# Attention and SoLU layer on one core: the output product with 16-bit words in place of 32-bit ones

## The chip, the cores and the metric

The kernel runs on one core of one Trainium2 chip. The metric is device microseconds of one execution, from the first to the last instruction and what lies around them. A run gives one time; the median of three runs stands for the kernel.

## The reference, cut to what matters

Eight batches of eight heads of causal attention with a decay (576 positions, head size 64) give `x`, 4608 tokens by 512. A layer follows, token by token:

```python
h = x @ w_in                      # 512 -> 1024
e = exp(h - max(h)); sm = e / (sum(e) + 1e-9)
solu = h * sm
ln = (solu - mean(solu)) / sqrt(var(solu) + 1e-6) * g_ln
out = ln @ w_out                  # 1024 -> 512
```

Inputs and output are 32-bit floats. `q` and `k` are scaled so that the scores spread widely, and the result must be near that of 32-bit arithmetic.

## The kernel before, in words

The 4608 tokens are 36 tiles of 128, called layers 0 to 35 here. The attention of eight batches, four pairs of heads each, feeds them through `xt`, a buffer of two batches. A layer (`layer`, L663) does this in order: TensorE multiplies `xh`, `xl` with `wi_h`, `wi_l` (L676 to L678, 24 matmuls of 512 columns into `hps`); VectorE takes the row's maximum (L687), ScalarE the exponential (L688), VectorE weighs and sums (L692 to L695), ScalarE squares for the variance (L700), GpSimd makes the inverse deviation in two small instructions (L704, L705), and the row is centred. The normalised row `z` must be transposed before the second product. Layers 5 to 29 (`turned`) have it as two 16-bit words, written by L318 and L714, transposed by DMA into `zz16` and then converted to two 32-bit words `zh` and `zl` by a ScalarE copy (L316, through `copied`) and a VectorE copy (L318), two halves each. Layers 0 to 4 and 30 to 35 transpose the 32-bit row on TensorE (L726) and split it on the way out of PSUM: `zh` by ScalarE (L734), `zl` by VectorE (L735). In these the row is only centred (L718); the inverse deviation is applied to the output (L776, L767), so that L718 does not wait for L705.

The second product (`product_out`, L743 to L745) takes three matmuls for each of eight blocks of 128 hidden units: `zh` with the high word of W_out, `zh` with its low word, `zl` with the high word; all operands are `float32r`, 128 by 128 stationary and 512 columns moving. That is 24 matmuls a layer. The last layer does it in two halves of 256 columns (L756, L757, L759).

W_out comes in as four tiles of 64-bit floats (`prepare_w_out`, L428; `weights`, L387): each is loaded, made into 32-bit floats by L409, L411 and a copy, and then every block of 128 rows is multiplied by its `g_ln` and split into `wo(0, k)` (through `copied`) and `wo(1, k)` (L439), block by block, as soon as its own tile is there. The 32-bit tile lies in `zt` or in a buffer of the attention (`w_buffer`). W_in goes through the same helper earlier.

The order on every engine is set once, when the program is built, by `Plan.schedule`: each operation has an engine, a cost in ns, a due time and keys that it reads and writes; of what is ready on an engine the one with the least due time goes first, within a short window (`WAIT`). Due times are a priority, not a clock. A matmul group needs a slot of PSUM: two each of `s` (scores), `t` (transposes), `o` (outputs). Engines run their order strictly; on the chip an instruction that waits holds back all behind it. All DMAs are issued by SyncE's queue (L322, L325). Where the plan leaves TensorE idle in its first 140 us and after 690 us, short 16-bit matmuls of a constant (L832, 256 columns) fill the time.

Of the kernel before, what the change touches and what calls it, by code (L numbers as in the profile page):

```python
# [18 lines left out]
P = 128  # L19
# [19 lines left out]
COLUMN, TRANSPOSE = 0.4525, 109.0  # L39
# [143 lines left out]
DUE = dict(load=-29.542, split=-28.082, upper=-25.473, v=-9.217, S=((-17.447, -8.873), (-8.986, -3.876), (-5.065, -1.009), (-2.23, 0.228), (-0.2, 2.951)), T=((-3.123,), (-2.859,), (2.11, 1.41), (11.821, 15.242), (13.671, -6.196, 17.385)), V=((15.498, 10.925), (22.811, 25.245)))  # L183
EARLY = dict(load=-47.636, split=-34.061, upper=-50.243, v=-30.564, S=((17.018, -28.783), (6.139, -25.484), (-23.782, -37.469), (19.88, -8.857), (6.983, 36.241)), T=((16.416,), (-36.513,), (8.628, 2.588), (20.731, -15.249), (-3.969, 15.962, 16.559)), V=((-14.112, -16.964), (35.156, 1.04)))
PAIR = 23.13
C_OUT = 56.244
START = 86.713
HALF = ((28.5, 0.126), (52.37, -6.098))
# [3 lines left out]
AT_P, AT_L = (-12.344, -0.643, -5.355, 1.678, 0.284, 4.447, 0.791, -2.369, 8.072, 3.467, 4.155, -6.961, 0.853, 3.12, 2.845, 2.503, -2.212, -3.177, 1.73, -1.504, 6.409, 1.012, 0.682, -2.76, -5.909, 3.11, -3.789, -9.069, -2.092, 8.061, -5.047, -4.728), (1.766, 17.998, -5.159, 17.233, 0.49, -2.325, -5.371, -4.319, -2.569, 0.3, 6.438, 6.85, -0.263, 5.808, -0.074, -4.855, -0.333, 0.475, 6.874, 4.872, 7.281, 9.093, -1.339, -8.226, -2.067, -5.356, -6.63, -2.031, -3.859, 16.597, -2.614, -2.295, 1.064, 4.109, 7.541, 10.907)  # L192
FIRST = 96.18

STAGES = (-7.935, 1.059, 6.086, 23.041, 12.213)
# [3 lines left out]
def tile_kernel(ctx: ExitStack, tc: tile.TileContext, qk, v, f, w_in, w_out, g_ln, out):  # L199
# [99 lines left out]
    st = [sb(f"st_{n}", 8) for n in range(2)]  # L299

# [86 lines left out]
    def weights(src, n, due, t, tk, w, wk, first=()):  # L387

        def words(x):
            return now(t).rearrange("p c (n t) -> p c n t", t=2)[:, :, :, x]  # L390
        dma(due + W_DMA[n // NCC] if n else -98, t, src.bitcast(I32).rearrange("p (c n) -> p c n", n=512), 712 if tk[0][0] != "xt" else 940, reads=first, writes=tk)
        w = w.rearrange("p (c n) -> p c n", c=4)
        wi = w.bitcast(I32)


        copied(W_UP[n], {ACT: 1140, POOL: 1150}, due, w, lambda: words(1).bitcast(F32), tk, [wk], scale=2.0 ** -112)
        for a in range(2):
# [8 lines left out]
            else:  # L406
# [10 lines left out]
    def prepare_w_in(c, due):  # L417
        w, wk = w_buffer(c % 3)
        weights(w_in[c], c, due, lambda: buf(f"wo_{c}", "raw", 4, DM, dtype=I32), [(("wo", "wol")[c // 2], 4 * (c % 2) + j) for j in range(4)],
                w, wk, summed if c else ())  # L420
        copied(WI_H[c], {ACT: 1050, DVE: 690, POOL: 1130}, due, wi_h[:, c, :], w, [wk], [("wi", c)])
        op(WI_L[c], 2360 if WI_L[c] == POOL else 1170, due, lambda: (nc.gpsimd if WI_L[c] == POOL else nc.vector).tensor_tensor(
            wi_l[:, c, :], w, wi_h[:, c, :].bitcast(F32), ALU.subtract), reads=[wk, ("wi", c)], writes=[("wil", c)], port=True)

    def wo(x, k):
        return buf(f"wo_{2 * x + k // 4}", "f32r", 4, DM, dtype=F32R)[:, k % 4, :]

    def prepare_w_out(c, due):  # L428
# [4 lines left out]
        w, wk = w_buffer(1 + c % 2)  # L433
        weights(w_out[c], NCC + c, due, t, tk, w, wk, summed)
        w = w.rearrange("p (r n) -> p r n", r=2)
        for r in range(2):
            k = 2 * c + r
            copied(WO_H[k], {ACT: 600, DVE: 400, POOL: 620}, due, lambda k=k: wo(0, k), w[:, r], [("g",), wk], [("wo", k)], scale=g_sb[:, k:k + 1])
            op(DVE, 650, due, lambda r=r, k=k: nc.vector.scalar_tensor_tensor(  # L439
                wo(1, k), w[:, r], g_sb[:, k:k + 1], wo(0, k).bitcast(F32), ALU.mult, ALU.subtract),  # L440
               reads=[("g",), wk, ("wo", k)], writes=[("wol", k)], port=True)


# [219 lines left out]
    def layer(n, at):  # L663
# [6 lines left out]
        s = st[n % 2]  # L670
# [32 lines left out]
        def deviation(by=2.0 ** -20 if turned else 1.0):  # L703
            nc.gpsimd.tensor_scalar(s[:, 6:7], s[:, 5:6], by / DFF, 1.0e-6 * by, ALU.mult, ALU.add)  # L704
            nc.gpsimd.tensor_tensor(s[:, 7:8], s[:, 6:7], mhalf, ALU.pow)  # L705
        op(POOL, 805, at if turned else at + 1.0, deviation, [("st5", n % 2)], [("st7", n % 2)])
# [8 lines left out]
        else:  # L715
            for a in range(2 if last else 1):
                sl, zk = (slice(512 * a, 512 * a + 512), ("z", a)) if last else (slice(0, DFF), ("z",))
                op(c_eng, {DVE: 360 if last else 690, POOL: 1200}[c_eng], at, lambda sl=sl: engine(c_eng).tensor_scalar(  # L718
                    zt[:, sl], et[:, sl], s[:, 4:5], 1.0, ALU.add, ALU.mult), [("e",), ("st", n % 2)], [zk], clear=[("z",)], port=c_eng == DVE)
        at += tz - tmid  # L720
        for a in range(2):
            key = ("t", "z", n, a)

            def turn(a=a, key=key):
                for k in range(4):
                    nc.tensor.transpose(ps_t[plan.place[key]][:, k, :], zt[:, (4 * a + k) * P:(4 * a + k + 1) * P], ident)  # L726
# [6 lines left out]
            op(PE, 4 * TRANSPOSE, at + 0.3 * a, turn, [("z", a) if last else ("z",)], [key], take=key, clear=[("zh", a), ("zl", a)])  # L733
            op(ACT, 470, at + 0.5, lambda a=a, key=key: nc.scalar.copy(zh[a], ps_t[plan.place[key]]), [key], [("zh", a)])  # L734
            op(DVE, 603, at + 1.0, lambda a=a, key=key: nc.vector.tensor_tensor(  # L735
                zl[a], ps_t[plan.place[key]], zh[a].bitcast(F32), ALU.subtract), [key, ("zh", a)], [("zl", a)])
# [3 lines left out]
        def product_out(k):  # L740
            o = ps_o[plan.place[key]]
            a, j = divmod(k, 4)
            nc.tensor.matmul(o, zh[a][:, j], wo(0, k), start=(k == 0), stop=False)  # L743
            nc.tensor.matmul(o, zh[a][:, j], wo(1, k), start=False, stop=False)  # L744
            nc.tensor.matmul(o, zl[a][:, j], wo(0, k), start=False, stop=(k == NFC - 1))  # L745

        if last:

            for b in range(2):
                ok, cols = ("o", "y", n, b), slice(256 * b, 256 * b + 256)  # L750

# [124 lines left out]
```

## Time and profile before

| | us |
|---|---|
| three runs, median | 795.7 |
| three runs, lowest and highest | 792.31, 798.37 |
| profiled execution, span from first to last instruction | 795.1 |
| TensorE busy | 780.0 |
| VectorE busy | 621.7 |
| ScalarE busy | 541.1 |
| GpSimd busy | 508.6 |

The profiled execution is one more execution with the profiler on; its span lies 0.6 us under the median of the runs. In the rows, PE is TensorE's matmuls, PEld its loads of the stationary operand, DVE VectorE, ACT ScalarE, POOL GpSimd, SP SyncE. A matmul's duration is its latency: matmuls overlap, so the time that one costs is the step from its start to the next one's start.

### The profile page before, as it was taken

The numbers are of one execution on the slowest core, as the hardware profiler recorded it, in microseconds if no ns is written. First come the engines' busy times: TensorE is split into PE (matmuls) and PEld (weight loads), VectorE is DVE, ScalarE is ACT, GpSimd is POOL, SyncE is SP. The second block draws the span as 40 slices with busy tenths as digits, with TensorE's granted clock in tenths as the row PEclk, the third lists the DMA queues.
The fourth block names the chain that finished last, engine by engine and source line by source line (L and its number), as shares of the span: only waits on it lengthen the run. The fifth ranks groups of instructions, "written<-read, shape, count | busy, mean of one in ns | idle before, by whom it ended". The sixth has DMA issues, their size and how long they took to land.

```text
span 795.1 us, 15849 instructions
## 1 busy us (share of the span) xinstructions
PE 780.0 (98%) x4763; PEld 660.6 (83%) x4763; DVE 621.7 (78%) x1902; ACT 541.1 (68%) x1367; POOL 508.6 (64%) x687
## 2 busy tenths in 40 slices
PE   8999999899999999999999999999999999999998
PEld 6667878788888888888888888888888888898887
DVE  6889878887878878988977878898879877885233
ACT  4565767876867777867766777776768776875343
POOL 4565667685668687758566787776767685752230
PEclk9899999999999999999999999999999999999999
DMA  8638577857476657766756666668476684520000
GB/s 269 202 115 233 156 195 201 217 163 192 120 184 152 159 147 188 181 148 164 181 148 165 148 168 152 159 159 205 122 194 137 153 181 123 118 49 14 27 27 27
DMA packets 117014, 120.08 MB, mean 151 GB/s; under 512 B 64000, under 2 KB 78592, under 8 KB 116160
## 3 DMA queue, kind: packets, MB, share of 16 engines
q1 hardware_dynamic: 116928, 119.06, 58.7%
q8 instruction: 38, 0.62, 0.4%
q14 instruction: 48, 0.39, 0.2%
HBM read 39.11 MB, written 10.03 MB: 62 GB/s over the span
## 4 chain that ended last, share of the span: by engine, by line
PE 85%; DVE 5%; DMA 3%; POOL 3%; issue 2%; ACT 1%; SPq 1%; POOLq 0%; DVEq 0%; ACTq 0%
PE ps_o L638 13%; PE ps_t L598 10%; PE hps L676 8%; PE ps_o L743 8%; PE hps L677 7%; PE hps L678 7%; PE ps_o L744 7%; PE ps_o L745 7%; PE ps L551 5%; PE ps L552 5%; PE hps L832 4%; DVE p L556 1%; POOL p L572 1%; PE ps_t L726 1%; PE ps L549 1%
## 5 line engine op out<-in xcount | busy, mean ns | idle before, releaser
L572 POOL TENSOR_SCALAR p<-p,ri 128x320 f32<-128x320 f32 (+4 forms) x320 | 191.1, 611 | 95.7 <-DVE ri L568 83.6
L559 ACT ACTIVATE p<-p,nm 128x320 f32<-128x320 f32 (+4 forms) x320 | 178.0, 557 | 68.2 <-DVE nm L556 60.7
L606 DVE TENSOR_TENSOR ptl_f32r<-ps_t,pth_f32r 128x384 fp32r<-128x384 f32 (+3 forms) x272 | 137.2, 519 | 23.5 <-ACT pth_f32r L316 20.9
L316 ACT ACTIVATE pth_f32r<-ps_t 128x384 fp32r<-128x384 f32 (+3 forms) x272 | 120.7, 461 | 51.2 <-PE ps_t L598 46.6
L556 DVE CUSTOM_DVE_ANT_0 p<-ps,mask 128x320 f32<-128x320 f32 (+4 forms) x320 | 130.6, 422 | 26.1 <-PE ps L552 11.7
L598 PE MATMUL ps_t<-ident,p 128*128 128x128 f32 x800 | 128.0, 275 | 3.6 <-DVE ptl_f32r L606 1.9
L598 PEld LDWEIGHTS ps_t<-ident,p 128*128 128x128 f32 x800 | 97.0, 141 | 28.0 <-POOL p L572 5.4
L676 PE MATMUL hps<-wi_h,xh 128*128 128x512 f32 x288 | 118.6, 412 | 0.0
L743 PE MATMUL ps_o<-wo_f32r,zh 128*128 128x512 f32 x280 | 117.3, 419 | 0.0
L677 PE MATMUL hps<-wi_l,xh 128*128 128x512 f32 x288 | 113.7, 395 | 0.0
L678 PE MATMUL hps<-wi_h,xl 128*128 128x512 f32 x288 | 113.6, 394 | 0.0
L551 PE MATMUL ps<-ks_f32r,qs_f32r 128*128 128x320 f32 (+3 forms) x360 | 110.5, 316 | 2.2 <-DVE nm L556 1.4
L744 PE MATMUL ps_o<-wo_f32r,zh 128*128 128x512 f32 x280 | 110.7, 396 | 0.0
L745 PE MATMUL ps_o<-wo_f32r,zl 128*128 128x512 f32 x280 | 110.5, 395 | 0.0
L552 PE MATMUL ps<-kz_f32r,qz 128*128 128x320 f32 (+3 forms) x360 | 102.9, 297 | 0.7 <-DMA kz_f32r<-raw 0.5
L638 PE MATMUL ps_o<-pth_f32r,vs_f32r 128*128 128x256 f32 (+1 forms) x368 | 94.4, 268 | 0.0
L672 POOL TENSOR_TENSOR xl<-xt,xh 128x512 fp32r<-128x512 f32 x36 | 46.5, 1293 | 57.5 <-ACT xh L671 56.7
L551 PEld LDWEIGHTS ps<-ks_f32r,qs_f32r 128*128 128x128 f32 (+1 forms) x360 | 65.0, 181 | 13.9 <-DVE nm L556 5.7
L638 PE MATMUL ps_o<-ptl_f32r,vs_f32r 128*64 128x256 f32 (+1 forms) x368 | 71.4, 264 | 0.0
L638 PEld LDWEIGHTS ps_o<-pth_f32r,vs_f32r 128*128 128x128 f32 x368 | 70.1, 191 | 1.6
L552 PEld LDWEIGHTS ps<-kz_f32r,qz 128*128 128x128 f32 (+1 forms) x360 | 65.3, 181 | 6.3 <-DMA kz_f32r<-raw 1.1
L678 PEld LDWEIGHTS hps<-wi_h,xl 128*128 128x128 f32 x288 | 54.1, 188 | 13.0
(137 smaller groups left out, 1611.6 us busy)
## 6 DMA issues: line engine op xcount, KB each, us to landing
raw<-in_qk_dram SPq DMA_DIRECT2D x64, 288.0 KB
ks_f32r<-hi SPq DMA_DIRECT2D x128, 144.0 KB
raw<-in_v_dram SPq DMA_DIRECT2D x32, 288.0 KB
kz_f32r<-raw SPq DMA_DIRECT2D x64, 144.0 KB
out_dram<-y SPq DMA_DIRECT2D x35, 256.0 KB
qs_f32r<-hi SPq DMA_DIRECT2D x56, 144.0 KB
qs_f32r<-raw SPq DMA_DIRECT2D x56, 144.0 KB
qz<-hi SPq DMA_DIRECT2D x56, 80.0 KB
```

The costliest lines, as they stand in the source:

```text
L551: nc.tensor.matmul(dst, qs(p)[:, h, q0:q0 + nq], ks(p)[:, h, cols], start=True, stop=False)
L552: nc.tensor.matmul(dst, z[:, h, z0:z0 + nq], kz(p)[:, h, cols], start=False, stop=True)
L559: op(ACT, E_NS[i], at + 1.3, lambda: nc.scalar.activation(pr, pr, AF.Exp, bias=x, scale=-1.0, accum_out=sm[m][i][:nq, h, 0:1]), [("nm", m, ...
L572: op(POOL, N_NS[i], at + 2.8, lambda g=g, pg=pg: nc.gpsimd.tensor_scalar(pg, pg, r_[:, g:g + 1], 1.0, ALU.mult, ALU.mult), [("ri", m, i)], ...
L598: nc.tensor.transpose(tp[:, s, :], pt[i][:, k * P:(k + 1) * P], ident)
L638: nc.tensor.matmul(o[:mm, a:w], vv, mv, start=(j == 0 and x == 0), stop=(j == order[-1] and x == 0))
L676: nc.tensor.matmul(hps[:, sl], xh[:, c, :], wi_h[:, c, sl], start=(c == 0), stop=False)
L677: nc.tensor.matmul(hps[:, sl], xh[:, c, :], wi_l[:, c, sl], start=False, stop=False)
L678: nc.tensor.matmul(hps[:, sl], xl[:, c, :], wi_h[:, c, sl], start=False, stop=(c == NCC - 1))
L743: nc.tensor.matmul(o, zh[a][:, j], wo(0, k), start=(k == 0), stop=False)
L744: nc.tensor.matmul(o, zh[a][:, j], wo(1, k), start=False, stop=False)
L745: nc.tensor.matmul(o, zl[a][:, j], wo(0, k), start=False, stop=(k == NFC - 1))
```

## The change

W_out's two words and z's two words become fp16. W_out times `g_ln` is scaled by a power of two that is found on the chip from its largest magnitude, the output copy divides by it (`scales`), and z is normalised in every layer before it is transposed, so L718 now reads the inverse deviation. The DMA-transposed words are used by the second product as they land: `zh`, `zl` and the two copies in layers 5 to 29 are gone, and `zz16` has two sets, of even and odd layers. W_out's four 32-bit tiles stay in memory until the scale is known: only then (`scale_w_out`, new) are the eight blocks scaled and split. Costs and due times of the planner are new throughout.

```diff
-COLUMN, TRANSPOSE = 0.4525, 109.0
+COLUMN, TRANSPOSE, SHORT = 0.4525, 109.0, 0.4215
...
-PAIR = 23.13
-START = 86.713
-W_IN, W_OUT, LOAD = (-14.581, 46.719), (174.062, 72.91), (87.19, -12.196)
-W_DMA = (-132.187, -51.852)
+PAIR = 23.152
+START = 86.674
+W_IN = (-31.427, 49.165)
+W_OUT = (167.026, 57.23)
+LOAD = (91.563, -22.285)
+W_SCALE = 216.178
+W_DMA = (-107.022, -70.722)
...
-    zh, zl = ([sb(f"z{x}_{a}", 4, P, dtype=F32R) for a in range(2)] for x in "hl")
-    zz16 = [sb(f"zz16_{a}", 2, 4, P, dtype=F16) for a in range(2)]
+    zz16 = [[sb(f"zz16_{m}_{a}", 2, 4, P, dtype=F16) for a in range(2)] for m in range(2)]
...
     def wo(x, k):
-        return buf(f"wo_{2 * x + k // 4}", "f32r", 4, DM, dtype=F32R)[:, k % 4, :]
+        return buf(f"wo_{2 + x}", "f16", NFC, DM, dtype=F16)[:, k, :]
...
-        w, wk = w_buffer(1 + c % 2)
-        weights(w_out[c], NCC + c, due, t, tk, w, wk, summed)
+        weights(w_out[c], NCC + c, due, t, tk, w, wk, summed, clear=[("raww", c // 2)])
+        op(DVE, 1200, due, lambda: nc.vector.tensor_reduce(
+            top[:, 2 * c:2 * c + 2], w().rearrange("p (r n) -> p r n", r=2), axis=AX.X, op=ALU.max, apply_absolute_value=True), [wk], [("top", c)])
+    def scale_w_out(due):
+        key = ("t", "scale")
+        def across():
+            nc.vector.tensor_tensor(top[:, :NFC], top[:, :NFC], g_sb, ALU.mult)
+            nc.vector.tensor_reduce(top[:, NFC:], top[:, :NFC], axis=AX.X, op=ALU.max, apply_absolute_value=True)
+        op(DVE, 320, due, across, [("g",), *(("top", c) for c in range(NFC // 2))], [("top",)])
+        op(PE, 150, due, lambda: nc.tensor.transpose(ps_t[plan.place[key]][:1, 0, :], top[:, NFC:], ident), [("top",), ("const",)], [key], take=key, dense=False)
...
+        op(DVE, 650, due, exponents, [key], [("scales",)])
+        op(PE, 150, due, lambda: nc.tensor.matmul(ps_t[plan.place[key]][:, 1, :2], ones, scales[:1, :], start=True, stop=True), [("scales",), ("ones",)], [key], dense=False)
...
+        op(DVE, 500, due, factors, [key, ("g",)], [("scales",), ("sg",)])
+        for k in range(NFC):
+            wk = ("w32", k // 2)
+            copied(WO_H[k], {ACT: 600, DVE: 400, POOL: 620}, due + k, lambda k=k: wo(0, k), lambda k=k: wo32(k), [("sg",), wk], [("wo", k)],
+                   scale=sg[:, k:k + 1], clear=[("raww", 2)])
+            op(DVE, 650, due + k, lambda k=k: nc.vector.scalar_tensor_tensor(
+                wo(1, k), wo32(k), sg[:, k:k + 1], wo(0, k), ALU.mult, ALU.subtract),
+               reads=[("sg",), wk, ("wo", k)], writes=[("wol", k)], clear=[("raww", 3)], port=True)
...
-        op(POOL, 805, at if turned else at + 1.0, deviation, [("st5", n % 2)], [("st7", n % 2)])
+        op(POOL, 805, at, deviation, [("st5", n % 2)], [("st7", n % 2)])
...
-                    zt[:, sl], et[:, sl], s[:, 4:5], 1.0, ALU.add, ALU.mult), [("e",), ("st", n % 2)], [zk], clear=[("z",)], port=c_eng == DVE)
+                    zt[:, sl], et[:, sl], s[:, 4:5], s[:, 7:8], ALU.add, ALU.mult), [("e",), ("st", n % 2), ("st7", n % 2)], [zk], clear=[("z",)], port=c_eng == DVE)
...
-                           [("z",), ("z", "l")], [("zz", a)])
-                copied(Z_ENG[2], {ACT: 560, DVE: 350, POOL: 600}, at + 0.5, zh[a], zz16[a][:, 0], [("zz", a)], [("zh", a)])
-                copied(Z_ENG[3], {ACT: 560, DVE: 350, POOL: 600}, at + 0.5, zl[a], zz16[a][:, 1], [("zz", a)], [("zl", a)])
+                           [("z",), ("z", "l")], zk)
...
-            nc.tensor.matmul(o, zh[a][:, j], wo(0, k), start=(k == 0), stop=False)
-            nc.tensor.matmul(o, zh[a][:, j], wo(1, k), start=False, stop=False)
-            nc.tensor.matmul(o, zl[a][:, j], wo(0, k), start=False, stop=(k == NFC - 1))
+            nc.tensor.matmul(o, zz[a][:, 0, j], wo(0, k), start=(k == 0), stop=False)
+            nc.tensor.matmul(o, zz[a][:, 0, j], wo(1, k), start=False, stop=False)
+            nc.tensor.matmul(o, zz[a][:, 1, j], wo(0, k), start=False, stop=(k == NFC - 1))
...
-            op(PE, 3 * 512 * COLUMN + 12, at + tout * k / 8, lambda k=k: product_out(k),
+            op(PE, 3 * 512 * SHORT, at + tout * k / 8, lambda k=k: product_out(k),
```

`exponents` is four VectorE instructions of one row, `factors` three small ones of 128 rows. The lists of due times (`DUE`, `EARLY`, `HALF`, `AT_P`, `AT_L`, `STAGES`) all have new values.

## Rows read from the trace of the kernel before

**Rows 1.** The page, part 1: busy time of each engine.

```profile
PE 780.0 (98%) x4763; PEld 660.6 (83%) x4763; DVE 621.7 (78%) x1902; ACT 541.1 (68%) x1367; POOL 508.6 (64%) x687
```

**Rows 2.** The page, part 4: the chain that ended last.

```profile
PE 85%; DVE 5%; DMA 3%; POOL 3%; issue 2%; ACT 1%; SPq 1%; POOLq 0%; DVEq 0%; ACTq 0%
```

**Rows 3.** Busy time by stretch: start:end length, PE, PEld, DVE, ACT, POOL, PEclk, DMA.

```profile
40.00:100.00 60.00, 59.14 (x378) 44.75 (x377) 51.72 (x144) 39.72 (x96) 37.26 (x52) 0.99 0.60 169
...
190.00:690.00 500.00, 497.18 (x3006) 427.18 (x3005) 413.68 (x1292) 361.45 (x933) 354.48 (x459) 1.00 0.65 159
742.00:786.00 44.00, 43.81 (x207) 35.51 (x206) 16.99 (x33) 18.21 (x31) 10.18 (x14) 1.00 0.05 19
```

**Rows 4.** Timeline of PE: from layer 32's output product to layer 34's input product.

```profile
755.24 0.40 PE L743 MATMUL ps_o<-wo_f32r,zh 128*128 128x512 f32 x1
...
760.14 0.40 PE L676 MATMUL hps<-wi_h,xh 128*128 128x512 f32 x1
```

**Rows 5.** Waits of PEld, 190 to 700 us: total, times, longest.

```profile
PEld ps_t L598 <- DVE ptl_f32r L606: 3.4, 8, 1.3
PEld ps L551 <- DVE nm L556: 3.4, 13, 0.8
```

**Rows 6.** Timeline of PE: 256 columns in 16-bit words, then in 32-bit ones.

```profile
66.57 2.68 PE L832 MATMUL hps<-ident 128*128 128x256 bf16 x23
...
412.47 0.28 PE L638 MATMUL ps_o<-pth_f32r,vs_f32r 128*128 128x256 f32 x1
...
412.82 0.28 PE L638 MATMUL ps_o<-ptl_f32r,vs_f32r 128*64 128x256 f32 x1
```

**Rows 7.** Instructions of line 832: ns min/median/max, first and last start.

```profile
L832 PE MATMUL hps<-ident x290: 270/273/421, 3.4 to 69.9; 128*128 128x256 bf16 x145
```

**Rows 8.** Instructions of line 743: ns min/median/max, first and last start.

```profile
L743 PE MATMUL ps_o<-wo_f32r,zh x280: 388/397/500, 99.5 to 783.6; 128*128 128x512 f32 x140
```

**Rows 9.** Groups by line and form: count, busy us, mean ns, idle before.

```profile
L687 DVE TENSOR_REDUCE st<-hps 128x1 f32<-128x1024 f32 x36 | 43.9, 1220 | 24.6 <-PE hps L678 24.3
...
L318 DVE TENSOR_SCALAR zl<-zz 128x512 fp32r<-128x512 f16 x50 | 32.5, 664 | 2.3 <-DMA zz<-z 1.9 <-PE ps_o L745 0.2
...
L316 ACT ACTIVATE zh<-zz 128x512 fp32r<-128x512 f16 x50 | 30.5, 627 | 11.1 <-DMA zz<-z 9.2 <-ACT e L688 1.0 <-PE ps_o L744 0.9
...
L695 DVE TENSOR_SCALAR st<-st 128x1 f32<-128x1 f32 x36 | 5.5, 154 | 1.5
```

**Rows 10.** Instructions of line 439: ns min/median/max, first and last start.

```profile
L439 DVE SCALAR_TENSOR_TENSOR wo_f32r<-ptl_w,g_sb,wo_f32r x4: 723/742/752, 58.1 to 77.0; 128x512 fp32r<-128x512 f32 x4
```

**Rows 11.** Timeline of all engines: the end of layer 34 and layer 35's chain.

```profile
775.62 0.69 DVE L735 TENSOR_TENSOR zl<-ps_t,zh 128x512 fp32r<-128x512 f32 x1 [4.32 <-ACT zh L734]
...
778.67 0.40 PE L743 MATMUL ps_o<-wo_f32r,zh 128*128 128x512 f32 x1
...
783.41 1.16 ACT L700 ACTIVATE p<-e,st 128x1024 f32<-128x1024 f32 x1 [2.01 <-DVE st L695]
783.48 0.88 DVE L718 TENSOR_SCALAR z<-e,st 128x512 f32<-128x512 f32 x2
...
784.28 1.03 PE L726 MATMUL ps_t<-ident,z 128*128 128x128 f32 x8
784.47 0.18 ACT L700 ACTIVATION_READ_ACCUMULATOR p<-e,st 128x1 f32 x1
...
784.74 0.19 POOL L704 TENSOR_SCALAR st<-st 128x1 f32<-128x1 f32 x1 [10.04 <-ACT p L700]
785.02 0.55 POOL L705 TENSOR_TENSOR st<-st,mhalf 128x1 f32<-128x1 f32 x1
...
785.84 0.39 PE L756 MATMUL ps_o<-wo_f32r,zh 128*128 128x256 f32 x1 [0.19 <-ACT zh L734]
```

**Rows 12.** Timeline of PE: layer 2's last output triple, layer 3's first.

```profile
181.58 0.48 PE L743 MATMUL ps_o<-wo_f32r,zh 128*128 128x512 f32 x1
...
194.28 0.39 PE L743 MATMUL ps_o<-wo_f32r,zh 128*128 128x512 f32 x1
```

More of the change, by code (lines that the diff above doesn't have):

```diff
@@ L198, in tile_kernel @@
+FIRST = 96.162
+STAGES = (1.419, 1.059, 4.523, 23.041, 11.635)
 @with_exitstack
@@ L383, in tile_kernel, with weights, w4, wi @@
     dma(-90, g_sb, g_ln, 4, writes=[("g",)])
-    def weights(src, n, due, t, tk, w, wk, first=()):
+    def weights(src, n, due, t, tk, w, wk, first=(), clear=()):
         def words(x):
             return now(t).rearrange("p c (n t) -> p c n t", t=2)[:, :, :, x]
+        def w4():
+            return now(w).rearrange("p (c n) -> p c n", c=4)
+        def wi():
+            return w4().bitcast(I32)
         dma(due + W_DMA[n // NCC] if n else -98, t, src.bitcast(I32).rearrange("p (c n) -> p c n", n=512), 712 if tk[0][0] != "xt" else 940, reads=first, writes=tk)
-        w = w.rearrange("p (c n) -> p c n", c=4)
-        wi = w.bitcast(I32)
-        copied(W_UP[n], {ACT: 1140, POOL: 1150}, due, w, lambda: words(1).bitcast(F32), tk, [wk], scale=2.0 ** -112)
+        copied(W_UP[n], {ACT: 1140, POOL: 1150}, due, w4, lambda: words(1).bitcast(F32), tk, [wk], scale=2.0 ** -112, clear=clear)
         for a in range(2):
@@ L418, in prepare_w_in @@
         w, wk = w_buffer(c % 3)
-        weights(w_in[c], c, due, lambda: buf(f"wo_{c}", "raw", 4, DM, dtype=I32), [(("wo", "wol")[c // 2], 4 * (c % 2) + j) for j in range(4)],
+        weights(w_in[c], c, due, lambda: buf(f"wo_{c}", "raw", 4, DM, dtype=I32), [("raww", c)],
                 w, wk, summed if c else ())
@@ L432, in prepare_w_out @@
             t, tk = buf("ptl_1", "raw", 256 * 9, dtype=I32)[:, :2048].rearrange("p (c n) -> p c n", c=4), [("ptl", 3), ("ptl", 4)]
-        w, wk = w_buffer(1 + c % 2)
-        weights(w_out[c], NCC + c, due, t, tk, w, wk, summed)
[L435 to L441, printed above, removed]
+        wk = ("w32", c)
@@ L763, in layer @@
                         for k in range(4 * a, 4 * a + 4):
[L764 to L765 removed]
+                            op(PE, (2 - x) * (256 * SHORT + 4), at + 3.0 * b + 0.1 * k, lambda k=k, x=x, product=product: product(k, x),
+                               [(("zh", "zl")[x], n % 2, a), ("wo", k)] if x else [("zh", n % 2, a), ("wo", k), ("wol", k)], [ok],
                                take=ok if k == 0 and x == 0 else None)
                 op(ACT, 360, at + 3.0 * b, lambda ok=ok, cols=cols: nc.scalar.activation(
[L768 removed]
+                    yt[:, cols], ps_o[plan.place[ok]][:, :256], AF.Copy, scale=scales[:, 0:1]), [ok, ("scales",)], [("y", b)], clear=[("y",)])
                 dma(at + 3.0 * b, out[n * P:(n + 1) * P, cols], yt[:, cols], 128, reads=[("y", b)])
@@ L771, in layer @@
         for k in range(NFC):
-            op(PE, 3 * 512 * COLUMN + 12, at + tout * k / 8, lambda k=k: product_out(k),
-               [("zh", k // 4), ("zl", k // 4), ("wo", k), ("wol", k)], [key], take=None if k else key)
+            op(PE, 3 * 512 * SHORT, at + tout * k / 8, lambda k=k: product_out(k),
+               [("zh", n % 2, k // 4), ("zl", n % 2, k // 4), ("wo", k), ("wol", k)], [key], take=None if k else key)
         at += tout
-        y = yt
-        op(ACT, 590, at, lambda: nc.scalar.activation(y, ps_o[plan.place[key]], AF.Copy, scale=2.0 ** -10 if turned else s[:, 7:8]),
-           [key, ("st7", n % 2)], [("y",)])
-        dma(at, out[n * P:(n + 1) * P, :], y, 256, reads=[("y",)])
+        op(ACT, 590, at, lambda: nc.scalar.activation(yt, ps_o[plan.place[key]], AF.Copy, scale=scales[:, 0:1]),
+           [key, ("scales",)], [("y",)])
+        dma(at, out[n * P:(n + 1) * P, :], yt, 256, reads=[("y",)])
     def half_of(p, half, at, due):
```

58 lines of the change are left out of this document (36 added, 22 removed).

## The prediction

> **What bounds the kernel now.** I read the busy times first: TensorE has 780.0 us of the 795.1 us span, VectorE 78% and the others less [rows 1]. Busy alone does not prove a bound here, since matmuls overlap, so the second view is the chain that ended last: 85% of it is TensorE, VectorE and DMA together 8% [rows 2]. The third is the table by stretch. Between 190 and 690 us TensorE is busy 497.2 of 500 us at full granted clock, VectorE 413.7, ScalarE 361.5, GpSimd 354.5; in the last stretch, after the attention has ended, TensorE is full and the others are mostly idle; only between 40 and 100 us does another engine come near, VectorE with 51.7 of 60 us [rows 3]. The fourth is the timeline, to see whether TensorE really streams: from 755.24 to 760.14 us there are 21 matmuls of 512 columns one after the other, 4.90 us, 233.3 ns each [rows 4]. Their latency of about 395 ns is not what they cost; the step is. The waits say the rest: what the loads of the stationary operand wait for VectorE between 190 and 700 us is 3.4 + 3.4 = 6.8 us in all [rows 5]. So from about 190 us on, a nanosecond off TensorE's steps is a nanosecond off the span; before that it is a matter of what else arrives.
>
> **The change, part by part.**
>
> *Output product.* 35 layers of 8 blocks run each of three lines 280 times (line 743's row: x280) [rows 8], 840 matmuls of 512 columns; the last layer adds 48 of 256. All change from 32-bit to 16-bit words. The trace has 16-bit matmuls, the fillers: 23 of them of 256 columns take 2.68 us, of which the last one's own latency is 0.27 us [rows 7], so 2.41 us / 22 = 109.5 ns a step [rows 6]. The 32-bit ones of 256 columns step 0.35 us / 3 = 116.7 ns [rows 6], and half of 233.3 is the same 116.7: the 32-bit cost goes by the column. If the 16-bit one goes by the column too, 512 cost 219.0 ns and 14.3 ns are saved; if it is a column per cycle at the granted 2.4 GHz (106.7 ns for 256) and 2.8 ns fixed, 216.1 ns and 17.2 ns. The upper end is 213.3 ns, cycles alone, 20.0 ns saved. I take 217 ns, 16.3 ns saved: 840 x 16.3 = 13.7 us and 48 x 7.2 ns = 0.35 us, 14.05 us in all (12.0 to 16.8). Not all of it shortens the span. Layers 0 to 2 are multiplied between 99.5 [rows 8] and 181.6 us [rows 12], where TensorE still waits now and then; I count half of their 72 x 16.3 ns as hidden, 0.6 us. Layer 34's product lies beside the last layer's chain on VectorE and ScalarE, which does not get shorter: 0.4 us hidden. That leaves -13.0 us.
>
> The Trainium skill (TensorE: Matmul & The Clock Gate, Back-to-back issue gap) gives 512 / 2.4 + 2.5 ns, 215.7 ns, for a matmul at the higher clock; 840 times 17.6 ns would be an estimate of 14.8 us. The fillers' 109.5 ns at 256 columns lie near its 109.2 ns; it says nothing of why the 32-bit ones step 17 ns wider.
>
> *z's copies in layers 5 to 29.* 50 ScalarE copies of 627 ns and 50 VectorE ones of 664 ns go [rows 9]: 31 and 33 us of work, 9% and 8% of what these engines do between 190 and 690 us [rows 3]. They are off TensorE's path, so the 31 and 33 us are not a gain. What they can give is a part of the waits that end on VectorE, at most 6.8 us [rows 5] and at least nothing, since a wait can pass to GpSimd's normalisation, which keeps its work. I take -3.0 us, a little under half. Each half of z is also ready one copy earlier, which nothing waits for while TensorE has other work.
>
> *W_out's preparation.* What is loaded, rebuilt and split is the same; ahead of the split come four maxima over 1024 elements, for which L687's 1220 ns is the nearest row, and nine small VectorE instructions near L695's 154 ns [rows 9]: 4.9 + 1.4 = 6.3 us more VectorE work, in a stretch where it is idle for 8.3 us of 60 [rows 3]. Two tiny TensorE operations wait between them. Behind the first, the transpose of the maxima, stands everything on TensorE if VectorE's maximum is late; the plan puts it where its input should be ready, and its due time of 216 lets almost anything go ahead. Between the two a slot of `t` is held, of which there are two; the attention's transposes would have one for a few us. The split used to follow each tile; now its 16 instructions stand behind the last tile. Before, the last low word was started at 77.0 us [rows 10] and first used after 99.5 us [rows 8], 22 us later. The new chain after the last tile is 1.2 us (maximum), some 3 us (scale, two crossings to TensorE), and eight low words of 0.742 us [rows 10], 5.9 us: 10 us if dense, 20 us if VectorE gives it every other slot. It fits, barely. The bounds are 0 (all in idle VectorE time) and +6.3 us (all exposed); I take +2.5, nearer to the lower end, as the stretch also waits for DMAs. The four W_out loads keep their size and their place behind `xt` and `ptl_1`; the 32-bit tiles no longer take `zt`, which frees a little, counted as nothing.
>
> *z normalised before the transpose (layers 0 to 4, 30 to 35).* L718 now waits for two small GpSimd instructions, 0.19 + 0.55 us [rows 11]. In layer 34 the first half's low word is ready at 775.62 + 0.69 = 776.31 us and used at 778.67 us, 2.4 us later [rows 11]: the delay of under 1 us is covered by the next layer's input product. What loses that cover is the last layer, with nothing behind it. Today its z starts at 783.48 us, beside the square (783.41); now it must wait for the square, its sum (784.65), and GpSimd's two, which end at 785.57. z's first half takes about half of L718's 0.88 us, so the transposes start near 786.2 instead of 784.28, and everything after them moves by 1.9 us [rows 11]. Bounds: 1.0 us if the plan finds an overlap, 2.3 if the crossing to VectorE is slow. I take +1.9 us.
>
> *Due times.* The whole order is new. Nothing in the trace prices it; I count nothing and widen the range.
>
> **Sum.** -13.0 - 3.0 + 2.5 + 1.9 = -11.6 us. From the span of 795.1 us that is 783.5 us; the median of the runs lies 0.6 us above the span, so 784.1 us. Within the forecast's own bounds: most gain -15.8 - 6.8 + 0 + 1.0 = -21.6 (774.1), least -11.0 - 0 + 6.3 + 2.3 = -2.4 (793.3).
>
> **The rivals.** (A measurement of this kernel tells about 1% from no change: below 787.7 us is faster, above 803.7 slower.)
>
> *W_out's words come late, one layer's product is displaced.* If they are ready only after 105 us or so, layer 0's 24 matmuls (24 x 217 ns = 5.2 us) leave a stretch that has room and are paid in one that has none: 784.1 + 5.2 = 789.3 us, the same within 1%. For it: the low priority and VectorE's load [rows 3]. Against it: 22 us of slack [rows 8, 10].
>
> *The width does not matter.* The step is set by something that both formats share, and the 16.3 ns do not appear: 784.1 + 13.0 = 797.1 us, the same. For it speaks that the fillers are 256 columns of a constant, not 512 of data, and that they ran where little else used the memory; against it the 116.7 against 109.5 ns [rows 6]. The Trainium skill (TensorE: Matmul & The Clock Gate, Weight-path perf modes) states that the array processes one element per cell per cycle regardless of the element's width, which would give just this; the trace's two steps at 256 columns differ by 7 ns, so it does not agree for 32-bit against 16-bit words.
>
> *Slower: the scale becomes a gate.* The chain over VectorE and TensorE gets its slots so late that the words are not there when layer 3 wants to multiply (194.3 us [rows 12]). Then the products of layers 0 to 2 are all displaced (15.6 us), the extra VectorE work is exposed in full (+3.8 over my value) and the relief is lost (+3.0): 784.1 + 22.4 = 806.5 us. The mechanism decides for slower from about the third displaced layer; with two it ends at 801 us. Against it: W_out's steps had low priority before too and were done by 77.7 us [rows 10].
>
> *Better than forecast.* All of the 6.8 us of waits go and the preparation hides: 784.1 - 3.8 - 2.5 = 777.8 us.
>
> **How the numbers follow.** Forecast 0.60 (nearly all of it faster), better 0.12, one layer displaced 0.14 (a quarter of it still under 787.7), width does not matter 0.07, gate 0.07. Faster 0.59 + 0.12 + 0.03 = 0.74; slower is the gate's 0.07 less the part of it with only two layers displaced, 0.06; the rest, 0.20, the same. The range that leaves out two in ten reaches from the better case's lower side to the forecast's upper bound: 775.5 to 793.0 us.
>
> **What would show it.** Right: the step of L743 to L745's successors near 217 ns while L676 to L678 stay at 233; no ScalarE or VectorE copy between the DMA transpose and the product; VectorE with some 33 us less work in a stretch like that of 190 to 690 us, about 381 of 500; the last split of W_out before the first output product, and that product near 100 us; the last layer's transposes about 2 us behind the square's end. Wrong: steps of 230 ns; a first output product past 110 us with fillers in its place; waits of TensorE's scale transpose or of attention transposes for a `t` slot; a granted clock below 1.00 after 60 us, which would double the cost of every step there; or waits on GpSimd that take up what VectorE gives back.

## The result and the profile after

The changed kernel took 784.23 us (median of 4 runs, 783.74 to 786.25) against 795.73 us: a ratio of 0.9858, 95% interval 0.9826 to 0.9889. The profiled execution has a span of 782.0 us, 13.1 us under that of before. The forecast was 784.1 us, faster. A time lies some 1.8 us above the span of its own execution (783.74 and 782.0 us here), so the profiled execution of the kernel before stands for about 796.9 us, 1.2 us above its median.

The page of the changed kernel, parts 1 and 4, answers to [rows 1, 2]:

```profile
PE 768.1 (98%) x4817; PEld 589.8 (75%) x4817; DVE 595.1 (76%) x1865; ACT 515.0 (66%) x1317; POOL 499.2 (64%) x688
...
PE 78%; DMA 8%; DVE 5%; SPq 3%; POOL 3%; issue 2%; ACT 1%; POOLq 0%; DVEq 0%; ACTq 0%
```

TensorE is as full as before; VectorE lost 26.6 us and ScalarE 26.1 us, less than the copies' 33 and 31. By stretch, the same view as [rows 3]:

```profile
40.00:100.00 60.00, 58.17 (x360) 41.32 (x358) 54.77 (x148) 36.80 (x90) 36.77 (x51) 1.00 0.67 189
...
190.00:690.00 500.00, 496.77 (x3090) 385.98 (x3089) 395.01 (x1281) 348.23 (x913) 348.02 (x462) 1.00 0.66 159
```

Between 190 and 690 us VectorE is 18.7 us lighter, not 33. In part that is because 2.8% more matmuls, and the work that belongs to them, now fit into the same 500 us (3090 against 3006). TensorE's timeline over layer 34's output product answers to [rows 4]:

```profile
765.86 0.38 PE L781 MATMUL ps_o<-wo_f,zz 128*128 128x512 f16 x1
...
771.04 0.27 PE L870 MATMUL ps_o<-ident 128*128 128x256 bf16 x1
```

Between these two starts lie 24 matmuls: 5.18 us / 24 = 215.8 ns each, where it was 233.3. The loads of the stationary operand between 190 and 700 us, as in [rows 5]:

```profile
PEld L781 <- issue: 4.9, 22, 0.3
PEld ps L590 <- DVE nm L595: 4.2, 17, 0.4
PEld L781 <- DMA zz<-z: 2.9, 4, 1.0
PEld ps_t L637 <- DVE ptl_f32r L645: 2.5, 8, 0.5
PEld ps_o L677 <- DVE xt L699: 1.9, 5, 0.6
```

Waits that end on VectorE are 8.6 us here (4.2 + 2.5 + 1.9). Before, the same three kinds were 7.3 us, the two lines of [rows 5] and this one:

```profile
PEld ps_o L638 <- DVE xt L660: 0.5, 2, 0.4
```

The product now waits four times for the DMA transpose itself. The end of the kernel, as in [rows 11]:

```profile
764.32 1.22 DVE L726 TENSOR_REDUCE st<-hps 128x1 f32<-128x1024 f32 x1 [6.27 <-PE hps L717]
764.75 1.07 ACT L772 CAST zz<-ps_t 128x512 f16<-128x512 f32 x2 [4.85 <-PE ps_t L765]
764.99 1.04 PE L870 MATMUL ps_o<-ident 128*128 128x256 bf16 x8
...
770.00 0.18 ACT L739 ACTIVATION_READ_ACCUMULATOR p<-e,st 128x1 f32 x1
...
770.54 0.55 POOL L744 TENSOR_TENSOR st<-st,mhalf 128x1 f32<-128x1 f32 x1
...
771.13 1.00 DVE L757 TENSOR_SCALAR z<-e,st 128x512 f32<-128x512 f32 x2 [2.22 <-POOL st L744]
...
773.07 0.28 PE L794 MATMUL ps_o<-wo_f,zz 128*128 128x256 f16 x1
```

z now starts after GpSimd's second small instruction (its wait, 2.22 us, names it). From the start of VectorE's maximum to the first output matmul this chain takes 773.07 - 764.32 = 8.75 us. Before, it started here and ended at 785.84 us [rows 11], 6.96 us later:

```profile
778.88 1.23 DVE L687 TENSOR_REDUCE st<-hps 128x1 f32<-128x1024 f32 x1 [1.43 <-PE hps L678]
```

W_out's scale chain, on all engines:

```profile
72.22 0.71 DVE L456 TENSOR_TENSOR top<-top,g_sb 128x8 f32<-128x8 f32 x1
...
73.18 0.27 PE L459 MATMUL ps_t<-ident,top 128*1 128x128 f32 x1 [0.24 <-DVE top L457]
...
75.02 0.38 PE L468 MATMUL ps_t<-scales,ones 1*128 1x2 f32 x2
...
75.75 0.23 DVE L473 TENSOR_SCALAR sg<-g_sb,scales 128x8 f32<-128x8 f32 x1
```

It takes 3.8 us, once. Then the instructions of the low words and of the product's first line, as in [rows 10, 8]:

```profile
L479 DVE SCALAR_TENSOR_TENSOR wo_f<-wo_f,sg,wo_f x8: 733/744/1153, 79.1 to 105.8; 128x512 f16<-128x512 f32 x8
```

```profile
L781 PE MATMUL ps_o<-wo_f,zz x280: 379/379/396, 87.5 to 770.4; 128*128 128x512 f16 x140
```

The last word comes at 105.8 us instead of 77.0, yet the first product starts at 87.5 us instead of 99.5: block by block it runs right behind the words, and layer 0's last output matmul starts at 108.4 us where it was 108.9.

Where the 13.1 us went is told by the steps. For every matmul I took the time from its start to the next one's start; columns times 0.4525 ns (32-bit), times 0.4215 ns (16-bit) and 109 ns per transpose are its work, the early unsplit 32-bit matmuls count as measured, and what is left, with the fillers, is time without work. In us, for all profiled executions of this study:

```
                        output  other | without work       | ends | span
                        product work  | <190  -700  after  |      |
before                    200.1  511.5 |  54.9  20.0   1.7 |  6.9 |  795.1
after                     186.4  509.9 |  55.2  20.8   2.6 |  7.2 |  782.0
e8_shift                  186.4  509.8 |  56.3  22.0   2.5 |  6.9 |  783.8
e6_old_dues               186.4  511.0 |  58.2  23.2   4.7 |  6.9 |  790.3
e7_before_new_dues        200.1  509.8 |  61.7  32.8   3.7 |  6.9 |  814.9
e13_before_light          200.1  510.7 |  54.7  20.0   1.7 |  6.9 |  794.1
e2_copies16               186.4  509.8 |  64.5  32.8   5.9 |  6.9 |  806.3
e1_words32                200.1  509.8 |  64.2  31.6   6.1 |  6.9 |  818.6
e10_copies16_old_dues     186.4  512.1 |  64.6  32.9   6.0 |  6.9 |  808.8
e5_load_back              186.4  509.8 |  56.1  39.7   3.7 |  6.9 |  802.6
e11_load_act              186.4  509.8 |  56.2  36.0   2.9 |  7.2 |  798.5
e12_load_dve              186.4  509.8 |  56.3  33.4   3.6 |  6.9 |  796.4
e3_late_norm              186.4  509.8 |  55.3  21.0   2.0 |  7.2 |  781.7
e9_tail                   186.4  509.8 |  55.3  19.9   1.6 |  7.2 |  780.1
```

The 13.7 us between 200.1 and 186.4 follow from these two costs per column; the measured steps of 233.3 and 215.8 ns would give 14.7 us and 0.4 for the last layer. The time without work is the same to within 1 us in each stretch. So at first sight the lighter ScalarE and VectorE, W_out's scale and the new due times did nothing. Two things show that this is not so: the granted clock, and the experiments.

**The granted clock.** By stretch, in the columns of [rows 3], the kernel before has

```profile
20.00:40.00 20.00, 18.95 (x119) 13.69 (x119) 16.04 (x47) 9.93 (x33) 11.53 (x15) 0.87 0.65 200
40.00:60.00 20.00, 19.89 (x121) 13.25 (x120) 17.21 (x57) 13.57 (x39) 13.36 (x21) 0.96 0.40 118
140.00:200.00 60.00, 57.82 (x371) 50.61 (x370) 50.31 (x174) 45.97 (x124) 40.81 (x58) 0.97 0.71 191
```

and the changed kernel has 1.00 in all three, as in

```profile
20.00:40.00 20.00, 19.89 (x148) 14.63 (x147) 15.37 (x47) 10.53 (x33) 12.19 (x17) 1.00 0.65 200
```

With the two levels of 2.4 and 1.2 GHz the means of before say that about 10 us ran at the lower one (2 x (0.13 x 20 + 0.04 x 20 + 0.03 x 60) = 10.4 us). In such a stretch the 32-bit matmuls of 256 columns step 0.64 us / 3 = 213 ns, where [rows 6] has 116.7:

```profile
156.17 0.41 PE L638 MATMUL ps_o<-pth_f32r,vs_f32r 128*128 128x256 f32 x1
...
156.81 0.41 PE L638 MATMUL ps_o<-ptl_f32r,vs_f32r 128*64 128x256 f32 x1
```

In the table this is most of the 1.6 us by which the other work fell, and 2.2 of the 54.9 us: by so much the matmuls at the lower clock exceed their work. With these 3.8 us put down to the clock, the rest of the account is: product -13.7, time without work before 190 us +2.5 (55.2 against 52.7), from 190 to 700 us +0.8, after that +0.9, ends +0.3, together -9.2 us. In the experiments, the 13 executions of the kernel before with a mean granted clock of 0.999 or more have a median of 791.99 us and the other 32 one of 794.85 us, and all four of the changed kernel had 0.999 or more, so at equal clock the change is worth about 7.8 us, not 11.5. Why the clock fell in one kernel and not in the other was not tested.

### The profile page after: what moved, and what is told of

Read it like the earlier page. It is cut to its first block, busy times and chain, and to the rows that moved or that the text cites. A ratio compares the mean times of both kernels' runs of the same rounds, so it can differ in the third digit from the quotient of the medians.

```text
span 782.0 us, 15882 instructions
## 1 busy us (share of the span) xinstructions
PE 768.1 (98%) x4817; PEld 589.8 (75%) x4817; DVE 595.1 (76%) x1865; ACT 515.0 (66%) x1317; POOL 499.2 (64%) x688
## 4 chain that ended last, share of the span: by engine, by line
PE 78%; DMA 8%; DVE 5%; SPq 3%; POOL 3%; issue 2%; ACT 1%; POOLq 0%; DVEq 0%; ACTq 0%
PE ps_o L677 12%; PE ps_t L637 10%; PE ps_o L781 7%; PE hps L715 7%; PE hps L716 7%; PE hps L717 7%; PE ps_o L782 7%; PE ps_o L783 7%; PE ps L590 5%; PE ps L591 5%; SPq L326 3%; DMA zz<-z 2%; DMA wo_raw<-in_w_in_dram 1%; DVE p L595 1%; PE ps_t L765 1%
## 5 line engine op out<-in xcount | busy, mean ns | idle before, releaser
L611 POOL TENSOR_SCALAR p<-p,ri 128x448 f32<-128x448 f32 (+4 forms) x320 | 183.1, 588 | 92.3 <-DVE ri L607 72.6
L598 ACT ACTIVATE p<-p,nm 128x192 f32<-128x192 f32 (+4 forms) x320 | 177.8, 557 | 63.7 <-DVE nm L595 54.1
L595 DVE CUSTOM_DVE_ANT_0 p<-ps,mask 128x192 f32<-128x192 f32 (+4 forms) x320 | 130.5, 422 | 30.7 <-PE ps L591 22.6
L637 PE MATMUL ps_t<-ident,p 128*128 128x128 f32 x800 | 124.6, 274 | 1.4 <-POOL p L611 0.7
L590 PE MATMUL ps<-ks_f32r,qs_f32r 128*64 128x64 f32 (+4 forms) x360 | 120.0, 344 | 1.0 <-DVE nm L595 0.5
L781 PE MATMUL ps_o<-wo_f,zz 128*128 128x512 f16 x280 | 107.4, 384 | 1.9 <-DMA zz<-z 1.8
L782 PE MATMUL ps_o<-wo_f,zz 128*128 128x512 f16 x280 | 106.1, 379 | 1.1 <-DVE wo_f L479 1.1
L783 PE MATMUL ps_o<-wo_f,zz 128*128 128x512 f16 x280 | 106.1, 379 | 0.0
L591 PE MATMUL ps<-kz_f32r,qz 128*64 128x64 f32 (+4 forms) x360 | 103.5, 295 | 0.0
L677 PE MATMUL ps_o<-pth_f32r,vs_f32r 128*128 128x128 f32 (+1 forms) x368 | 95.1, 272 | 0.0
L677 PE MATMUL ps_o<-ptl_f32r,vs_f32r 128*64 128x128 f32 (+1 forms) x368 | 71.8, 262 | 0.0
L726 DVE TENSOR_REDUCE st<-hps 128x1 f32<-128x1024 f32 x36 | 43.9, 1220 | 31.4 <-PE hps L717 30.9
```

The costliest lines, as they stand in the source:

```text
L590: nc.tensor.matmul(dst, qs(p)[:, h, q0:q0 + nq], ks(p)[:, h, cols], start=True, stop=False)
L591: nc.tensor.matmul(dst, z[:, h, z0:z0 + nq], kz(p)[:, h, cols], start=False, stop=True)
L598: op(ACT, E_NS[i], at + 1.3, lambda: nc.scalar.activation(pr, pr, AF.Exp, bias=x, scale=-1.0, accum_out=sm[m][i][:nq, h, 0:1]), [("nm", m, ...
L611: op(POOL, N_NS[i], at + 2.8, lambda g=g, pg=pg: nc.gpsimd.tensor_scalar(pg, pg, r_[:, g:g + 1], 1.0, ALU.mult, ALU.mult), [("ri", m, i)], ...
L637: nc.tensor.transpose(tp[:, s, :], pt[i][:, k * P:(k + 1) * P], ident)
L677: nc.tensor.matmul(o[:mm, a:w], vv, mv, start=(j == 0 and x == 0), stop=(j == order[-1] and x == 0))
```

## The experiments

Each ran 5 to 12 times against the kernel before on the same chip. The changed kernel was not run again beside them: differences from its 784.2 us are taken across sessions, in which the kernel before had medians from 793.9 to 795.7 us.

**The width alone.** e1 and e2 undo the removal of the copies; e1 undoes the 16-bit words too, and computes with half of W_out. Their planned order is one.

```diff
-    turned_dma(..., zz[a] ..., zk)
+    turned_dma(..., zd(a) ..., [("zd", a)])
+    copied(Z_ENG[2], ..., zz[a][:, 0], zd(a)[:, 0], [("zd", a)], zk[:1])
+    copied(Z_ENG[3], ..., zz[a][:, 1], zd(a)[:, 1], [("zd", a)], zk[1:])
...
-    return buf(f"wo_{2 + x}", "f16", NFC, DM, dtype=F16)[:, k, :]
+    return buf(f"wo_{2 + x}", "f32r", 4, DM, dtype=F32R)[:, k % 4, :]   # e1 only
```

> The changed kernel with one part undone: z's two words are copied once more by ScalarE and VectorE after the DMA transpose in layers 5 to 29, into one set of buffers, and stay 16-bit. Theory (the copies were off TensorE's path and their removal gave nothing, since waits that end on VectorE did not fall between 190 and 700 us): 782 to 787 us, that is the changed kernel's 784.2 within the 3 us that any new order may cost. Rival (their removal was worth 3 us or more, as predicted): 787 to 791 us.

> The changed kernel with two parts undone: z's two words are copied once more by ScalarE and VectorE after the DMA transpose (layers 5 to 29, one set of buffers), and all words of the output product are 32-bit again. Blocks 4 to 7 of W_out's words take the place of blocks 0 to 3, for want of memory, so the output product computes with half of W_out. Its planned order is that of e2_copies16, with the same costs, so the two differ in the width of the words alone. Theory (the gain is the step of the output product, 233.3 against 215.8 ns): 840 x 17.5 ns = 14.7 us and 0.4 for the last layer over e2_copies16, less about 1 us hidden in the first 190 us and beside the last layer's chain: e2_copies16 + 14 us, 796 to 801 us. Rival (the width is worth little, the gain comes from the new order and the lighter engines): less than 7 us over e2_copies16.

e2 took 811.37 us (ratio 1.0214, 1.0188 to 1.0241), e1 824.82 us (1.0391, 1.0365 to 1.0418). The width is worth 13.5 us between them, as the theory said, though e1's own forecast of 796 to 801 us fell with e2's. Their spans differ by 12.3 us; e2's profiled execution had a mean granted clock of 0.995 and e1's one of 1.000, which makes this difference smaller by up to 4.0 us (0.005 x 806.3). But e2's own number contradicts the theory on the copies and lies beyond the rival's range too: 27 us above the changed kernel, of which the lower clock is a part. Both kernels also key W_out's words by `k % 4`, so a block waits for two words; part of the 9.3 us that e2 lost before 190 us may be that, and this part stays open.

**The load of the copies, in an order that does not move.**

```diff
+            for _ in range(2 if TURNED[0] <= n < TURNED[1] else 0):    # layers 5 to 29
+                nc.vector.tensor_scalar(idle(0), mask[:, :512], 1.0, 1.0, ALU.mult, ALU.mult)
...
+            for _ in range(2 if turned else 0):
+                nc.scalar.activation(idle(1), mask[:, :512], AF.Copy, scale=1.0)
```

> The changed kernel in its own order on every engine, with the load of the removed copies put back and nothing else: in layers 5 to 29 two ScalarE copies of 128x512 behind the square and two VectorE ones behind the weighing write a buffer that nothing reads. Theory (the lighter engines give TensorE nothing): 784.2, within 1.5 us. Rival (the relief is worth the 3 us that were predicted, or more): 787 us or more. If the copies stand in a chain that TensorE waits for, the waits on VectorE's L595 and L645 grow and the time with them; that would say that the relief is real and was used by the new order.

> As e5_load_back (the changed kernel in its own order), with the two ScalarE copies alone in layers 5 to 29, 31 us of ScalarE work. e5_load_back took 804.8 us, 20.6 more than the changed kernel, and its loads of TensorE waited for VectorE's L598 and L648 where they had not. Theory A (VectorE's 24 us stand in front of what TensorE waits for, ScalarE's do not): 784 to 788 us. Theory B (ScalarE's copy out of PSUM comes late and VectorE's subtraction with it): 796 us or more. If both engines count, the two parts add up to about 20 us.

> As e5_load_back, with the two VectorE copies alone in layers 5 to 29, 24 us of VectorE work at 483 ns each. Theory A: 800 to 805 us, nearly all of the 20.6 us. Theory B: 784 to 790 us. If both count, the excess over 784.2 of this one and of e11_load_act add up to about 20 us.

Both loads: 804.83 us (1.0140, 1.0118 to 1.0162), 20.6 above the changed kernel, far into the rival's range. ScalarE's alone: 800.28 us (1.0084, 1.0065 to 1.0102), 16.0 above; VectorE's alone: 798.68 us (1.0065, 1.0045 to 1.0085), 14.5 above. ScalarE's number is theory B's, VectorE's lies 1.3 us under theory A's and far from B's, so neither theory holds: each engine alone costs most of it, and the parts do not add up, since 16.0 + 14.5 is 10 more than 20.6. The loads of the stationary operand in e5, between 190 and 700 us, show where it arrives:

```profile
PEld ps_t L640 <- DVE ptl_f32r L648: 12.2, 25, 1.3
PEld ps L593 <- DVE nm L598: 11.1, 32, 1.1
PEld ps_o L680 <- DVE xt L702: 5.5, 9, 1.5
```

8.6 us of such waits have become 28.8. With ScalarE's copies alone they are nearly the same three:

```profile
PEld ps L593 <- DVE nm L598: 10.3, 27, 1.0
PEld ps_o L680 <- DVE xt L702: 6.3, 8, 1.5
PEld ps_t L640 <- DVE ptl_f32r L648: 6.0, 10, 1.4
```

VectorE is named although only ScalarE was loaded. L648 and L702 read what ScalarE has copied out of PSUM, and between 190 and 700 us VectorE's wait for the first of these copies (L648 for L323) is 30.0 us here, 22.9 in the changed kernel; L598 does not read ScalarE's copy, it stands behind such lines in VectorE's order. TensorE has two slots of each kind, and of a burst of 0.97 or 1.25 us (2 x 483, 2 x 623 ns) on either engine about half comes through (14.5 and 16.0 us over 25 layers); that the two slots set this share was not tested. Nor was the load tried where the copies had been: e5 puts it elsewhere, two instructions at a time, so 20.6 us is the price of such bursts in this order, not shown to be that of the copies.

**The copies taken out of the old order.** The reverse of e5, in the order of the kernel before: all four copies cut to 2 columns of each 128 in layers 6 to 29.

```diff
-  ... zh[a], zz16[a][:, 0], ...
+  ... zh[a][:, :, :P if n == TURNED[0] else 2], zz16[a][:, 0, :, :P if n == TURNED[0] else 2], ...
```

> The kernel before in its own order on every engine, with the four copies of z's words cut to 2 columns of each 128 in layers 6 to 29, so that most of ScalarE's 31 and VectorE's 33 us are gone and nothing stands elsewhere; the words in those layers are then partly those of layer 5. It measures what the removal is worth where the order does not change. Theory (in an order that has a place for the copies they cost TensorE only a part of its 20 us of waits between 190 and 700 us; e5_load_back's 20.6 us came from an order that had no place for them): 0 to 5 us less than the kernel before. Rival (the copies cost about what e5_load_back and e10_copies16_old_dues suggest): 10 us or more less.

792.50 us, ratio 0.9970 (0.9948 to 0.9992): 2.3 us less, as the theory said. What is left of them, by groups and forms of that kernel:

```profile
L318 DVE TENSOR_SCALAR zl<-zz 128x8 fp32r<-128x8 f16 x48 | 16.7, 366 | 1.2 <-DMA zz<-z 1.0
L316 ACT ACTIVATE zh<-zz 128x8 fp32r<-128x8 f16 x48 | 9.1, 206 | 10.0 <-DMA zz<-z 9.0 <-PE ps_o L744 0.7 <-ACT e L688 0.2
```

Against 664 and 627 ns [rows 9] that is 48 x 298 ns = 14.3 us of VectorE and 48 x 421 ns = 20.2 us of ScalarE, about half of the load, for 2.3 us. The trace shows none of it where the copies stand: the time without work between 190 and 700 us is 20.0 us in both kernels. The 1.0 us between their spans is other work and time before 190 us, and e13's profiled execution had a clock of 0.996 against 0.994, so a part of the 2.3 us may be the clock. Where the order has a place for the copies, they cost TensorE little or nothing; where it has none (e5), a load of 24.1 + 31.2 us costs 20.6 us.

**The due times.**

```diff
-START = 86.674
+START = 86.9        # e8_shift
```

> The changed kernel with one due time moved: START 86.9 instead of 86.674, so that pairs 4 to 31 of the attention are due 0.23 us later against the layers; costs and operations as they are. It is the control for every kernel whose order was planned anew without a search. Theory (the due times that were searched are worth some 10 us, and any other order loses most of that): 788 us or more. Rival (the order is robust, and the times of e2, e6 and e10 are due to their operations): 783 to 786 us.

> The changed kernel with the due times of the kernel before (scale_w_out keeps 216.178), all else as changed. Theory (the 16-bit step gives its 14 us in any order, the lighter engines give little in an order that was made for heavier ones): 782 to 787 us. Rival (the gain needs the new due times, since an order is only good for the costs that it was searched for): 790 us or more, by waits of TensorE between 190 and 700 us above 20 us.

> The kernel before with the due times of the changed one, no other edit: the part 'due times searched anew' alone. Theory (due times are good for the costs that they were searched with, no better in themselves): 800 to 815 us, slower than before. Rival (the new due times are simply better): 785 to 795 us.

> e2_copies16 (16-bit words, but z's two words copied once more after the DMA transpose) with the due times of the kernel before, which were made for these copies. e2_copies16 took 811.4 us under the new due times. Theory (a planned copy costs nothing where the order has a place for it): within 4 us of e6_old_dues, so that the removal of the copies alone gives nothing. Rival (the copies take what TensorE needs once it is 14 us faster): e6_old_dues + 10 us or more, near 795 us or above, so that the 16-bit words would give nothing without the removal.

The small shift gave 785.73 us (0.9899, 0.9871 to 0.9928), 1.5 above the changed kernel: the rival, an order of this kind is robust to a little. All due times put back: 796.04 us (1.0029, 1.0007 to 1.0050), the rival, no faster than the kernel before although its output product is 13.7 us shorter. Its profiled execution had a clock of 1.00 and spans 790.3 us, 8.3 more than the changed kernel's 782.0 us: at equal clock this, and not the 11.8 us between the medians, is what the due times are worth. The new due times on the kernel before: 816.40 us (1.0289, 1.0257 to 1.0322), 21.6 above it and a little over the theory's range. So neither list is better in itself; each fits the operations and costs that it was made for. Copies, 16-bit words and old due times together: 810.56 us (1.0207, 1.0181 to 1.0233), 14.5 above e6, the rival. This need not contradict e13: the planner's costs and W_out's operations are the new ones here, so the order is not the old one either.

**The tail.**

```diff
-   zt[:, sl], et[:, sl], s[:, 4:5], s[:, 7:8], ALU.add, ALU.mult)
+   zt[:, sl], et[:, sl], s[:, 4:5], 2.0 ** 20 if last else s[:, 7:8], ALU.add, ALU.mult)
...
-   yt[:, cols], ps_o[...][:, :256], AF.Copy, scale=scales[:, 0:1])
+   yt[:, cols], ps_o[...][:, :256], AF.Copy, scale=s[:, 6:7])   # inverse deviation * scale
...
-AT_L = (..., 0.375)
+AT_L = (..., 10.28)    # e9 only
```

> The changed kernel with one part undone in the last layer alone: its z is centred and scaled by a constant power of two, and the inverse deviation goes into the output copy's scale, so that z does not wait for GpSimd's two instructions. The order is planned anew. Theory (the last layer's chain from the end of its input product to its first output matmul grew from 6.96 to 8.75 us and lies bare at the end): 1.8 us less than the changed kernel, 782.4 us, and that chain near 7 us again. Rival (the tail is set by the other layers' products): no change, 784.2 us. A new order can blur either by some 2 us, so the chain's length decides.

> e3_late_norm with AT_L's last value 10.28 instead of 0.375: layer 35's input product is due later, so that layer 34's eight transposes stand between its matmuls, as in the kernel before, and the eight fillers behind them are gone; nothing else in TensorE's order moves. In e3_late_norm the last layer's z was ready at 769.8 us, but TensorE was in layer 34's output product until 771.3. Theory (TensorE's own 0.9 us of fillers before that product held the end): 0.9 us less than e3_late_norm, and 1.0 to 1.3 less than the changed kernel: 783.1 us. Rival (the end is set by the output copies and their DMA): no change, 784.1 us.

e3 took 784.06 us (0.9878, 0.9856 to 0.9900), no change, the rival. The timeline of its end:

```profile
764.59 1.23 DVE L726 TENSOR_REDUCE st<-hps 128x1 f32<-128x1024 f32 x1 [6.26 <-PE hps L717]
...
769.28 0.88 DVE L757 TENSOR_SCALAR z<-e,st 128x512 f32<-128x512 f32 x2
...
771.31 1.04 PE L769 MATMUL ps_t<-ident,z 128*128 128x128 f32 x8
...
772.78 0.28 PE L798 MATMUL ps_o<-wo_f,zz 128*128 128x256 f16 x1
```

z starts 1.8 us sooner, but its transposes stand behind layer 34's output product and start 0.4 us sooner: the chain is 8.19 us, not 7. e9 moves that product forward and takes 783.79 us (0.9872, 0.9844 to 0.9900), with a span of 780.1 against 782.0 in single executions. That is 0.4 us less in the median, too little for these intervals. No version was shown to beat the changed kernel.

## Why the prediction was right

The main mechanism was right: TensorE's step in the output product sets the gain. That the number fits to 0.1 us is in part luck. A forecast gain of 3.0 us did not come, and 3.8 us came from a term that the forecast does not have, the granted clock.

*Output product.* Right in mechanism and nearly in size: 217 ns were taken, 215.8 measured, 17.5 ns less on each of 840. That is 14.7 us with 0.4 for the last layer, against 14.05; the table's costs and e1 against e2 give 13.7 and 13.5 where 13.0 was the net forecast. The Trainium skill gives 512 / 2.4 + 2.5 = 215.8 ns for the isolated gap (TensorE: Matmul & The Clock Gate, Back-to-back issue gap), and the trace agrees with its 215.8; the about 131 ns that the same section gives for a stream of loads and matmuls are not reached here. Its rule that the element's width does not matter (Weight-path perf modes) does not hold between 32-bit and 16-bit words here, 233.3 against 215.8 ns at 512 columns.

*Relief of ScalarE and VectorE, -3.0.* This term failed. The working counted 6.8 us of waits on VectorE; with a third kind they were 7.3, and they went to 8.6, and the time without work from 20.0 to 20.8. In the old order e13 took about half of the load away for 2.3 us, and its trace shows the same 20.0. What the working missed is that a faster TensorE asks more of the others, 2.8% more matmuls in the same 500 us; that the copies' place paid for this is argued, not shown. e5 shows only that the new order has no room for such a load: 20.6 us are lost.

*W_out's preparation, +2.5.* The costs were right (four maxima of 1208 ns, the chain 3.8 us; the first small instruction took 0.71 us where 0.15 was assumed, the bare minimum of the rest). The time without work before 190 us is 55.2 against 54.9 us, but 2.2 of the 54.9 are slower steps at the lower clock, so at equal clock 2.5 us more show there. The size fits; whether the preparation or the order made it was not separated. The rival of a displaced product did not come: the last word was late, at 105.8 us, but the product ran behind the words from 87.5 us.

*The last layer, +1.9.* Right as a chain: from VectorE's maximum to the first output matmul 8.75 us against 6.96, 1.8 more. Of that, 0.9 us shows as time without work after 700 us. e3 showed why it cannot be had back alone: TensorE's own order stands at the same place.

*Due times, nothing.* This was the step that could have broken the forecast. With the old due times the changed kernel is at 796.0 us, and its span at a clock of 1.00 is 8.3 us longer: most of the gain hangs on the order. The forecast priced the operations as if the order would be as good as before, and it was.

*The clock, not in the sum.* The forecast started from a profiled execution with some 10 us at the lower clock before 200 us and took that as given. [Rows 3] shows 0.99 from 40 to 100 us; the 0.87 from 20 to 40 us and the 0.97 from 140 to 200 us do not enter the working. In the changed kernel the clock stays at 1.00, which is 3.8 us of the 13.1 between the spans. The sum's 0.6 us from span to time also joins two different executions; within one it is 1.8 us.

## What to carry to other kernels

Where one engine streams without gaps, price a change by that engine's step from start to start, and look in the same trace for an instruction of the new type: a filler of 256 columns gave this step to within 1%. Before two times are compared, compare the granted clock of both profiles stretch by stretch: here it went with a third of the difference between the medians. A statically planned order is part of the kernel: an operation that costs next to nothing where it has a place can cost a third to three fifths of its time on the bound engine where it has none (e5, e11, e12), and a part of a change tried without a new plan can look like no gain or a loss. To separate an operation from its order, keep the order and change the operation (e1 against e2, e5, e13).

## What was not expected of the hardware

Loads on two engines that feed the same two slots do not add: 16.0 and 14.5 us apart, 20.6 together. A VectorE copy cut from 512 elements to 8 still took 366 ns on the mean (664 before), while ScalarE's cut copy took 206 ns. The trace of e13 shows what such a small VectorE instruction waits for: the 11 of its 48 copies that started while GpSimd was idle took 152 to 173 ns, and of the 22 that took over 200 ns, up to 1404, 21 ended 21 to 32 ns after the GpSimd instruction that was running when they started. The VectorE product of 8 columns in the scale chain (L456, 0.71 us from 72.22) stood beside such an instruction too, and ended 0.02 us after it:

```profile
72.17 0.74 POOL L530 TENSOR_TENSOR raw<-raw,hi 128x256 fp32r<-128x256 f32 x1
```

So the 154 ns of a small VectorE instruction [rows 9] are its price only while GpSimd does not hold it up.
